# Parameter tables of a state-space convolution built in two halves of the channels, with new instruction lists

## The chip, the cores and the metric

The kernel runs on one core of one Trainium2 chip. The core has five engines that each work through their own row of instructions in order: TensorE (PE, matmuls; the loads of its weights are shown as PEld), VectorE (DVE), ScalarE (ACT), GpSimd (POOL) and SyncE (SP, which here only issues DMA transfers; ACT issues some too). An engine that reaches an instruction whose semaphore has not been raised stands still, with all that is behind it. The metric is the device time of one execution in microseconds; lower is better.

## What is computed

Two independent heads read different inputs of 2048 positions by 448 channels, and their outputs stand side by side. The first is a linear attention of 16 heads with softmax features:

```python
phi_q = jnp.concatenate([_softmax(pq, axis=-1), _softmax(-pq, axis=-1)], axis=-1)
phi_k = jnp.concatenate([_softmax(pk, axis=-1), _softmax(-pk, axis=-1)], axis=-1)
kv = jnp.einsum("bhsf,bhsd->bhfd", phi_k, v)
z  = jnp.einsum("bhsf->bhf", phi_k)
...
o = num / den
```

The second is a state-space convolution. Each of the 448 channels has 256 complex states; they give a convolution kernel of 2048 taps, which is applied through Fourier transforms:

```python
dt = jnp.exp(log_dt)[:, None]
A = A_re + 1j * A_im
...
logdA = dt * A
dB = dt * Bc
...
P = jnp.exp(logdA[:, :, None] * l[None, None, :])
K = jnp.einsum("dn,dnl,dn->dl", Cc, P, dB).real
...
Yf = Uf * Kf[None, :, :, :]
y = (lambda x, s, axes=(-2,-1): jnp.fft.irfft2(x, s=s, axes=axes).astype(jnp.bfloat16))(Yf, (1, L2), axes=(-2, -1))[:, :, 0, :L]
y = (lambda x, *d: x.transpose(*d))(y, 0, 2, 1) + u * Dskip[None, None, :]
```

## The kernel before, in words

**Parameters.** The six raw parameter arrays (A, B, C; real and imaginary) are loaded as bf16 tiles of 112 partitions by 4 x 256 (`raw`, line 260). The 448 channels are split as (u p j): u is the half of the channels (224 each), p the partition, j one of two neighbours. `to_states` (331) multiplies them on PE with the diagonal matrix `DG` of time steps, which also turns them so that the 128 partitions hold states; the results go to a pair of PSUM banks, one for each half of the states. From A come `AT` and `TH` (340 to 349, in two bf16 parts each, by a copy and a difference), and in fp32 the powers of the decay: five exponentials (`amp`), ten sines (`cs`), five products (`PW`, 379) for the powers 128, 16, 8, 32 and 64, and the power 256 by squaring. From B and C come four products of 112 x 1024 (353) and from these the coefficients `CR`, the row for tap 0 (`K0`), and `CB` (`TM`, 389, is the product that it is made of). Each of these instructions covers all 448 channels: 896 columns for each of the real and the imaginary part.

**Tables by quarters.** The rest of the convolution runs in four quarters qt of 112 channels, 224 columns (`QC`). `tables(qt)` makes rotations (sines on ACT), dampings (exponentials on ACT), `hi_tables` and `damp` and `far` (products on DVE), then `build_k` (896 small matmuls over the four quarters) makes the taps, which are sent through DRAM (`scatter_k`) to another layout. `kernel_spectrum(qt)` transforms them on PE, and `conv(qt)` multiplies them on DVE with the signal's spectrum (`prod`, `finish`), transforms back on PE (`inverse`) and writes out.

**Signal and attention.** `signal_spectrum(b)` (419) mirrors u on PE with the constant `REV` (part of the tile `PID`), adds and subtracts on DVE (427, 428), and transforms on PE with the constants `G1`. `key_side` and `query_side` are the attention; they read x transposed by DMA (`xT`), and weights folded by `fold_weights`.

**What sets the order.** The program is collected as a list of some thousand operations, then issued in the order of a fixed list, `ORDER`. Three more lists fix where each tile stands in SBUF (`PLACES`, in units of 64 bytes), which PSUM banks a job uses (`SLOTS`), and which of two engines takes an operation that either could do, or which queue a DMA goes to (`PICKS`: A for ACT and V for DVE; S for SP and Q for ACT's queue). Tiles whose places overlap are kept apart by semaphores: a load into a place waits until the readers of what stood there are done, and whatever is behind it on SP waits too.

Of the kernel before, what the change touches and what calls it, by code (L numbers as in the profile page):

```python
# [19 lines left out]
SSM_N = 256  # L20
# [109 lines left out]
def kernel(  # L130
# [129 lines left out]
    raw = {nm: sb([112, 4, SSM_N]) for nm in srcs}  # L260

    def load_raw(nm):
        dma("S", raw[nm].rearrange("p (u j) n -> p u (j n)", u=2), srcs[nm].rearrange("(u p j) n -> p u (j n)", u=2, j=2))
# [15 lines left out]
    def load_u(b):  # L279
# [9 lines left out]
    prog.add("S", lambda: nc.scalar.dma_start(  # L289
        out=raw["Are"].rearrange("p (u j) n -> p u (j n)", u=2),  # L290
        in_=srcs["Are"].rearrange("(u p j) n -> p u (j n)", u=2, j=2)))
    dma("S", PID, P_d)
    for nm in ("Aim", "Cre", "Bre", "Cim", "Bim"):
        load_raw(nm)
# [30 lines left out]
    def from_states(bs):  # L325
        return view(psum[:, bs[0], 0:1], [512 * (bs[1] - bs[0]), 2], [56, 8], [1, 56])

    def by_states(v):
        return view(v, [56, 2], [112, 8], [1, 56])

    def to_states(bs, terms):
        items = []
        for j in range(4):
            for nch in range(2):
                at = 224 * (j // 2) + 56 * (j % 2)
                o = view(psum[:, bs[nch], at:at + 1], [112, 2], [1, 56])
                items += acc(o, [(t[:, j, 128 * nch:128 * nch + 128], d[:, j, :]) for t, d in terms])
        mms(items)

    AT = sb([128, 2, NCOL])  # L340
    TH = sb([128, 2, NCOL])
    bA, bT = prog.banks(2), prog.banks(2)
    for nm, b, dst in (("Are", bA, AT), ("Aim", bT, TH)):
        to_states(b, [(raw[nm], DG)])
        for nch in range(2):
            o0, o1 = (view(dst[:, part, 56 * nch:56 * nch + 1], [112, 8], [1, 2], [2, 28]) for part in range(2))
            i = view(psum[:, b[nch], 0:1], [56, 8], [28, 2], [1, 28])
            copy(o0, i)
            sub(o1, i, o0)
    prods = {}  # L350
    for a, b in (("Cre", "Bre"), ("Cim", "Bim"), ("Cre", "Bim"), ("Cim", "Bre")):
        prods[a + b] = sb([112, 4, SSM_N])
        mul(prods[a + b], raw[a], raw[b])

    LOWP = (128, 16, 8, 32, 64)
    PW = {k: sb([128, 2, NCOL]) for k in (8, 16, 32, 64, 128, 256)}
    amp = {k: sb([128, NCOL], F32) for k in LOWP}
    cs = {k: sb([128, 2, NCOL], F32) for k in LOWP}
    q128, q256 = (sb([128, 2, NCOL], F32) for _ in range(2))
    CR = sb([128, 2, NCOL])  # L360
    K0 = sb([128, D_MODEL])
    ones = sb([128, 128])
    for k in LOWP:
        af(by_states(amp[k]), from_states(bA), ACT.Exp, scale=float(k))
    for part, terms in enumerate(([("CreBre", DG), ("CimBim", DGN)], [("CreBim", DG), ("CimBre", DG)])):
        bs = prog.banks(2)
        to_states(bs, [(prods[n], d) for n, d in terms])
        copy(by_states(CR[:, part, :]), from_states(bs))
    mset(ones, 2.0 ** -17)
    (b_,) = prog.banks(1)  # L370
    mms([it for qt in range(4) for it in acc(
        view(psum[:, b_, 112 * qt:112 * qt + 1], [14, 8], [7, 2], [1, 7]),
        [(ones, view(CR[:, 0, QC * qt + 56 * nch:QC * qt + 56 * nch + 1], [7, 8], [112, 2], [1, 7]))
         for nch in range(2)])])
    copy(K0, psum[:, b_, 0:D_MODEL])
    for k in LOWP:
        af(by_states(cs[k][:, 0, :]), from_states(bT), ACT.Sin, scale=float(k), bias=bias_hp)
        af(by_states(cs[k][:, 1, :]), from_states(bT), ACT.Sin, scale=float(-k if k == 8 else k))
        mul(PW[k] if k != 128 else q128, cs[k], amp[k].unsqueeze(1).to_broadcast([128, 2, NCOL]))
        if k == 128:  # L380
            copy(PW[128], q128)
    s2 = sb([128, 2, NCOL], F32)
    square(s2, q128)
    sub(q256[:, 0, :], s2[:, 0, :], s2[:, 1, :])
    stt(q256[:, 1, :], q128[:, 0, :], -2.0, q128[:, 1, :], ALU.mult, ALU.mult)
    copy(view(PW[256][:, 0, 0:1], [56, 32], [1, 2], [2, 28]), view(q256[:, 0, 0:1], [56, 32], [28, 2], [1, 28]))
    CB = sb([128, 2, NCOL])
    TM = sb([128, 2, 2, NCOL])
    mul(TM, CR.unsqueeze(1).to_broadcast([128, 2, 2, NCOL]), PW[8].unsqueeze(2).to_broadcast([128, 2, 2, NCOL]))
    add(CB[:, 0, :], TM[:, 0, 0, :], TM[:, 1, 1, :])  # L390
    sub(CB[:, 1, :], TM[:, 0, 1, :], TM[:, 1, 0, :])
# [79 lines left out]
    def args(src, qt):  # L471
        cols = slice(qt * QC, (qt + 1) * QC)
# [23 lines left out]
    def dampings(qt):  # L496
        A = sb([128, 21, QC])
        p0, far_ = args(AT, qt)
# [13 lines left out]
    def damp(W, A, T, qt, x0, w):  # L512
        scaled(A[:, 2:21:3, x0:x0 + w], A[:, 1:20:3, x0:x0 + w], -1.0)
        for part in (1, 0):
            copy(view(W[:, part, 1, x0:x0 + 1], [56, w // 56], [2, 28], [1, 2]),
                 view(PW[8][:, part, qt * QC + x0:qt * QC + x0 + 1], [56, w // 56], [1, 28], [28, 2]))
            mul(view(W[:, part, 2, x0:x0 + 1], [2 * QC, 7], [QC, 2], [1, w]),
                view(A[:, 0, x0:x0 + 1], [3 * QC, 7], [(1 + part) * QC, 2], [1, w]),
                view(T[:, part, 0, x0:x0 + 1], [QC, 7], [0, 2], [1, w]))

    def far(W, qt, x0, w):
        def pw(i, n):
            return view(PW[256][:, i, qt * QC + x0:qt * QC + x0 + 1], [0, 2], [0, n], [1, w])
# [14 lines left out]
        def squares(s0, ka, kb, d0):  # L538
# [3 lines left out]
            for i in range(2):  # L542
# [4 lines left out]
             PW[256][:, :, qt * QC + x0:qt * QC + x0 + w])  # L547
# [6 lines left out]
    def hi_tables(qt):  # L554
        cols = slice(qt * QC, (qt + 1) * QC)
# [5 lines left out]
        copy(U_[:, :, 0], CB[:, :, cols].rearrange("p i (s x) -> p s i x", x=28))  # L561
        for k, n, s0, d0 in ((16, 1, 0, 1), (32, 2, 0, 2), (64, 4, 0, 4)):
            t = sb([128, 2, 8, n, 2, 28])
            for i in range(2):
                times(t[:, i], U_[:, :, s0:s0 + n], PW[k][:, i, cols], 2 * n)
# [3 lines left out]
        for i, o in ((1, t), (0, U_[:, :, 8:16])):  # L569
            times(o, U_[:, :, 0:8], PW[128][:, i, cols], 16)  # L570
# [153 lines left out]
    def kernel_spectrum(qt, tiles):  # L724
        sk = SK[qt]
        for m in range(0, 8, 2):
            for b in range(2):
                (bk,) = prog.banks(1)
                items = []
                for cp in range(2):  # L730
                    for k in range(2):
# [3 lines left out]
                            halves(K0[:, 112 * qt:112 * qt + 112]),  # L735
# [206 lines left out]
```

## Time and profile before

| what | us |
|---|---|
| median of 3 runs (232.2 to 234.28) | 232.46 |
| the profiled execution | 233.31 |
| its span on the page | 231.6 |
| what lies around the span | 1.71 |

The page gives 7313 instructions in 231.6 us, and three engines near their full time: PE 201.2 us (87%), DVE 211.5 (91%), ACT 195.2 (84%). The granted PE clock is below full only between 23 and 35 us. Rows of the busy table by stage show, behind the stretch and its length, busy time and number of instructions for each engine. Rows in order of time show the start, the busy time, the engine, the line, the operation with its shapes, and in brackets the idle time just before and what ended it. Rows of groups show shape and count, then total busy time and the mean of one in ns, then idle time before them. Most lines are helpers: 186 is any DVE operation on two tensors, 206 an activation, 214 a copy on either engine, 229 a matmul, 249 a DMA.

### The profile page before, as it was taken

To read this page: it belongs to the slowest core of one execution; us is meant where nothing else is said; L and a number is where in the kernel's file an instruction comes from. 1 tells how busy PE (TensorE), PEld (TensorE's weight loads), DVE (VectorE), ACT (ScalarE), POOL (GpSimd) and SP (SyncE) were. 2 spreads that over 40 slices of the span, in tenths; PEclk is the share of its full clock that TensorE was granted. 3 is DMA by queue.
4 is the path that set the end of the run, shared out by engine and by line. 5 is a ranking of instruction groups with operands and counts; after the bars stand their busy time and mean duration, and the time that the engine had idled before them with its cause. 6 is when DMAs were issued, how large, how long until landed. Compare 5 with 4: busy or idle time off the path is not lost.

```text
span 231.6 us, 7313 instructions
## 1 busy us (share of the span) xinstructions
PE 201.2 (87%) x3125; PEld 146.0 (63%) x3136; DVE 211.5 (91%) x268; ACT 195.2 (84%) x354; POOL 8.0 (3%) x26
## 2 busy tenths in 40 slices
PE   1115699999999999999886899999999998999994
PEld 1014345656556755797664877745667876789994
DVE  1469999999999999999999999999999996999990
ACT  3977999999999999999999999999699867445331
POOL 4000000000000200002000000010000000000000
PEclk9999569999999999999999999999999999999999
DMA  5918990536828949997755807124799239464173
GB/s 168 214 24 188 290 219 3 128 105 200 215 55 135 229 110 232 143 170 204 238 134 63 233 0 237 32 55 24 181 267 285 52 58 217 86 107 93 25 181 79
DMA packets 78247, 32.87 MB, mean 142 GB/s; under 512 B 64856, under 2 KB 76168, under 8 KB 77960
## 3 DMA queue, kind: packets, MB, share of 16 engines
q1 hardware_dynamic: 72840, 29.76, 59.7%
q10 hardware_dynamic: 5376, 2.65, 4.6%
q8 instruction: 24, 0.39, 0.8%
q14 instruction: 7, 0.06, 0.1%
HBM read 15.84 MB, written 8.49 MB: 105 GB/s over the span
## 4 chain that ended last, share of the span: by engine, by line
PE 58%; ACT 24%; issue 4%; DVE 4%; DVEq 0%; ACTq 0%
PE psum L229 57%; ACT sbuf L206 12%; ACT sbuf L214 11%; DVE sbuf L186 3%; ACT L206 1%; PE psum L239 1%; DVE sbuf L214 0%; DVEq L214 0%; ACTq L214 0%; DVEq L186 0%; ACTq L206 0%
## 5 line engine op out<-in xcount | busy, mean ns | idle before, releaser
L229 PE MATMUL psum<-sbuf 128*128 128x112 bf16 (+9 forms) x3077 | 199.0, 256 | 26.7 <-DVE sbuf L186 10.4
L186 DVE TENSOR_TENSOR sbuf<-sbuf 128x896 bf16<-128x896 bf16 (+11 forms) x214 | 190.9, 955 | 10.4 <-DMA sbuf<-in_B_u_dram 4.6
L229 PEld LDWEIGHTS <-sbuf 128*128 128x128 bf16 (+5 forms) x3088 | 143.5, 113 | 81.1 <-issue 22.6
L214 ACT CAST sbuf<-psum 128x448 bf16<-128x448 f32 (+8 forms) x124 | 79.6, 691 | 21.7 <-PE psum L229 19.1
L206 ACT ACTIVATE sbuf<-psum 128x512 bf16<-128x512 f32 (+6 forms) x154 | 83.1, 625 | 3.2 <-DVE sbuf L186 1.3
L206 ACT ACTIVATE sbuf<-sbuf 128x896 bf16<-128x896 bf16 (+3 forms) x29 | 18.8, 680 | 2.5 <-DMA sbuf<-in_B_log_dt_dram 1.3
L214 DVE CAST sbuf<-psum 128x448 bf16<-128x448 f32 (+4 forms) x21 | 12.2, 597 | 6.3 <-PE psum L229 6.2
L206 ACT ACTIVATE sbuf<-psum,sbuf 128x896 f32<-128x896 f32 (+3 forms) x17 | 13.7, 811 | 1.8 <-DVE sbuf L186 1.3
L224 POOL MEMSET sbuf<- 128x224 bf16 (+7 forms) x21 | 7.6, 388 | 157.1 <-PE psum L229 68.6
L214 ACT COPY sbuf<-psum 112x896 bf16<-112x896 bf16 (+2 forms) x12 | 7.1, 620 | 2.4 <-PE psum L239 1.9
L203 ACT ACT_TABLE_LOAD x5 | 6.4, 1283 | 1.3 <-PEq L926 1.3
L206 ACT ACT_TABLE_LOAD x4 | 5.1, 1283 | 0.1
L214 DVE COPY sbuf<-sbuf 128x448 bf16<-128x448 bf16 (+2 forms) x13 | 4.1, 319 | 0.0
L239 PE MATMUL psum<-sbuf 112*112 112x112 bf16 (+1 forms) x48 | 3.4, 216 | 0.7 <-DVE sbuf L186 0.7
L239 PEld LDWEIGHTS <-sbuf 112*112 112x112 bf16 (+1 forms) x48 | 2.9, 120 | 1.3 <-DVE sbuf L186 0.8
L186 DVE TENSOR_TENSOR sbuf<-psum,sbuf 128x448 bf16<-128x448 f32 (+1 forms) x6 | 2.8, 489 | 0.0
L214 DVE CAST sbuf<-sbuf 128x1792 bf16<-128x1792 f32 (+1 forms) x4 | 2.8, 710 | 0.0
L217 DVE TENSOR_SCALAR sbuf<-sbuf 128x1568 bf16<-128x1568 bf16 x4 | 2.5, 628 | 0.0
L214 ACT COPY sbuf<-sbuf 128x224 bf16<-128x224 bf16 (+1 forms) x5 | 2.2, 443 | 0.0
L220 ACT ACTIVATE sbuf<-sbuf 128x1792 f32<-128x1792 f32 x1 | 1.7, 1702 | 0.0
L217 ACT ACTIVATE sbuf<-sbuf 112x448 bf16<-112x448 bf16 x1 | 0.6, 577 | 0.8 <-DVE sbuf L309 0.8
L198 DVE SCALAR_TENSOR_TENSOR sbuf<-sbuf,psum 128x128 f32<-128x128 f32 x4 | 1.1, 285 | 0.0
(8 smaller groups left out, 2.5 us busy)
## 6 DMA issues: line engine op xcount, KB each, us to landing
SUd<-sbuf SPq DMA_DIRECT2D x8, 448.0 KB, 3.6
sbuf<-SUd SPq DMA_DIRECT2D x4, 896.0 KB, 4.9
sbuf<-const SPq DMA_DIRECT2D x8, 384.0 KB, 3.8
sbuf<-in_B_u_dram SPq DMA_DIRECT2D x4, 448.0 KB, 6.6
out_dram<-sbuf SPq DMA_DIRECT2D x13, 112.0 KB, 2.7
out_dram<-sbuf SPq DMA_DIRECT2D x3, 448.0 KB, 3.5
sbuf<-const SPq DMA_DIRECT2D x2, 512.0 KB
sbuf<-const ACTq DMA_DIRECT2D x1, 1024.0 KB
```

Source lines behind the costliest of these rows:

```text
L186: prog.add("V", lambda: nc.vector.tensor_tensor(out=o, in0=a, in1=b, op=op))
L198: prog.add("V", lambda: nc.vector.scalar_tensor_tensor(out=o, in0=a, scalar=s, in1=b, op0=op0, op1=op1))
L203: nc.scalar.preload_act_table_set("natural_log_exp_and_others")
L206: nc.scalar.activation(o, a, fn, **kw)
L214: either(lambda: nc.scalar.copy(o, a), lambda: nc.vector.tensor_copy(o, a))
L217: either(lambda: nc.scalar.activation(o, a, ACT.Copy, scale=s), lambda: nc.vector.tensor_scalar_mul(o, a, s))
L220: either(lambda: nc.scalar.activation(o, a, ACT.Square), lambda: nc.vector.tensor_tensor(out=o, in0=a, in1=a, op=ALU.mult))
L224: prog.add("G", lambda: nc.gpsimd.memset(o, v))
L229: nc.tensor.matmul(o, lhsT=l, rhs=r, **kw)
L239: nc.tensor.transpose(o, i, idn)
```

## The change

Everything from the raw loads to `CB` becomes a function of the half u, with tiles half as wide, and is called twice. The work of the second half stands behind in the lists. The two halves of the states now lie side by side in one PSUM bank instead of in a pair, so that the exponentials, sines and copies read plain rows. The quarters read the half `qt // 2`. The four lists are new; they also change places, banks, engines and order of operations that the rest of the diff does not touch: `PID` stands at 3415 instead of 370.

```diff
-    raw = {nm: sb([112, 4, SSM_N]) for nm in srcs}
...
+    raw = [{nm: sb([112, 2, SSM_N]) for nm in srcs} for u in range(2)]
...
     for nm in ("Aim", "Cre", "Bre", "Cim", "Bim"):
-        load_raw(nm)
+        load_raw(nm, 0)
+    for nm in srcs:
+        load_raw(nm, 1)
...
+    def to_states(b, u, terms):
+        mms([it for j in range(2) for nch in range(2) for it in acc(
+            view(psum[:, b, 112 * j + 56 * nch:112 * j + 56 * nch + 1], [224, 2], [1, 56]),
+            [(t[:, j, 128 * nch:128 * nch + 128], d[:, 2 * u + j, :]) for t, d in terms])])
...
+    HC = NCOL // 2
+    AT, TH, CR, CB = ([sb([128, 2, HC]) for u in range(2)] for _ in range(4))
+    PW = {k: [sb([128, 2, HC]) for u in range(2)] for k in (8, 16, 32, 64, 128, 256)}
+    K0 = [sb([128, D_MODEL // 2]) for u in range(2)]
...
+    def powers(u):
+        (bA,), (bT,) = prog.banks(1), prog.banks(1)
...
+            prods[a + b] = sb([112, 2, SSM_N])
+            mul(prods[a + b], raw[u][a], raw[u][b])
...
+        for k in LOWP:
+            af(amp[k], psum[:, bA, 0:HC], ACT.Exp, scale=float(k))
...
+        for k in LOWP:
+            af(cs[k][:, 0, :], psum[:, bT, 0:HC], ACT.Sin, scale=float(k), bias=bias_hp)
+            af(cs[k][:, 1, :], psum[:, bT, 0:HC], ACT.Sin, scale=float(-k if k == 8 else k))
+            mul(PW[k][u] if k != 128 else q128, cs[k], amp[k].unsqueeze(1).to_broadcast([128, 2, HC]))
+            if k == 128:
+                copy(PW[128][u], q128)
...
+        TM = sb([128, 2, 2, HC])
+        mul(TM, CR[u].unsqueeze(1).to_broadcast([128, 2, 2, HC]), PW[8][u].unsqueeze(2).to_broadcast([128, 2, 2, HC]))
+        add(CB[u][:, 0, :], TM[:, 0, 0, :], TM[:, 1, 1, :])
+        sub(CB[u][:, 1, :], TM[:, 0, 1, :], TM[:, 1, 0, :])
+
+    powers(0)
+    powers(1)
...
-        p0, far_ = args(TH, qt)
+        p0, far_ = args(TH[qt // 2], qt)
```

In the changed program DVE has 287 operations instead of 268, ACT 372 instead of 354 and PE as many as before; ACT loads a table eleven times instead of nine.

More of the change, by code (lines that the diff above doesn't have):

```diff
@@ L288 @@
     prog.add("G", lambda: nc.gpsimd.affine_select(eye, eye, [[-1, 112]], ALU.is_equal, 0.0, base=0, channel_multiplier=1))
[L289 to L291 removed]
+    prog.add("S", lambda: nc.scalar.dma_start(out=raw_pair("Are", 0)[0], in_=raw_pair("Are", 0)[1]))
     dma("S", PID, P_d)
     for nm in ("Aim", "Cre", "Bre", "Cim", "Bim"):
[L294 removed]
+        load_raw(nm, 0)
+    for nm in srcs:
+        load_raw(nm, 1)
     for i in range(4):
@@ L323, in two @@
         return view(psum[0:parts, bs[0], 0:1], [512 * (bs[1] - bs[0]), 2], [1, D_MODEL])
[L325 to L347, printed above, removed]
+    def to_states(b, u, terms):
+        mms([it for j in range(2) for nch in range(2) for it in acc(
+            view(psum[:, b, 112 * j + 56 * nch:112 * j + 56 * nch + 1], [224, 2], [1, 56]),
+            [(t[:, j, 128 * nch:128 * nch + 128], d[:, 2 * u + j, :]) for t, d in terms])])
@@ new lines @@
+    LOWP = (128, 16, 8, 32, 64)
+    HC = NCOL // 2
+    AT, TH, CR, CB = ([sb([128, 2, HC]) for u in range(2)] for _ in range(4))
+    PW = {k: [sb([128, 2, HC]) for u in range(2)] for k in (8, 16, 32, 64, 128, 256)}
+    K0 = [sb([128, D_MODEL // 2]) for u in range(2)]
+    ones = sb([128, 128])
+    mset(ones, 2.0 ** -17)
+    def powers(u):
+        (bA,), (bT,) = prog.banks(1), prog.banks(1)
+        for nm, b, dst in (("Are", bA, AT[u]), ("Aim", bT, TH[u])):
+            to_states(b, u, [(raw[u][nm], DG)])
+            o0, o1 = (view(dst[:, part, 0:1], [56, 8], [1, 2], [2, 28]) for part in range(2))
+            i = view(psum[:, b, 0:1], [56, 8], [28, 2], [1, 28])
@@ L348 @@
             copy(o0, i)
             sub(o1, i, o0)
[L350 to L391, printed above, removed]
+        prods = {}
+        for a, b in (("Cre", "Bre"), ("Cim", "Bim"), ("Cre", "Bim"), ("Cim", "Bre")):
+            prods[a + b] = sb([112, 2, SSM_N])
+            mul(prods[a + b], raw[u][a], raw[u][b])
@@ new lines, in powers @@
+        amp = {k: sb([128, HC], F32) for k in LOWP}
+        cs = {k: sb([128, 2, HC], F32) for k in LOWP}
+        q128, q256 = (sb([128, 2, HC], F32) for _ in range(2))
+        for k in LOWP:
+            af(amp[k], psum[:, bA, 0:HC], ACT.Exp, scale=float(k))
+        for part, terms in enumerate(([("CreBre", DG), ("CimBim", DGN)], [("CreBim", DG), ("CimBre", DG)])):
+            (b,) = prog.banks(1)
+            to_states(b, u, [(prods[n], d) for n, d in terms])
+            copy(CR[u][:, part, :], psum[:, b, 0:HC])
@@ new lines, in powers @@
+        (b_,) = prog.banks(1)
+        mms([it for q in range(2) for it in acc(
+            view(psum[:, b_, 112 * q:112 * q + 1], [14, 8], [7, 2], [1, 7]),
+            [(ones, view(CR[u][:, 0, QC * q + 56 * nch:QC * q + 56 * nch + 1], [7, 8], [112, 2], [1, 7]))
+             for nch in range(2)])])
+        copy(K0[u], psum[:, b_, 0:D_MODEL // 2])
+        for k in LOWP:
[4 more added lines that the diff above has]
+                copy(PW[128][u], q128)
@@ new lines, in powers @@
+        s2 = sb([128, 2, HC], F32)
+        square(s2, q128)
+        sub(q256[:, 0, :], s2[:, 0, :], s2[:, 1, :])
+        stt(q256[:, 1, :], q128[:, 0, :], -2.0, q128[:, 1, :], ALU.mult, ALU.mult)
+        copy(view(PW[256][u][:, 0, 0:1], [56, 16], [1, 2], [2, 28]), view(q256[:, 0, 0:1], [56, 16], [28, 2], [1, 28]))
+        TM = sb([128, 2, 2, HC])
+        mul(TM, CR[u].unsqueeze(1).to_broadcast([128, 2, 2, HC]), PW[8][u].unsqueeze(2).to_broadcast([128, 2, 2, HC]))
+        add(CB[u][:, 0, :], TM[:, 0, 0, :], TM[:, 1, 1, :])
@@ L560, in hi_tables @@
         U_ = sb([128, 8, N_HI, 2, 28])
-        copy(U_[:, :, 0], CB[:, :, cols].rearrange("p i (s x) -> p s i x", x=28))
+        copy(U_[:, :, 0], CB[qt // 2][:, :, cols].rearrange("p i (s x) -> p s i x", x=28))
         for k, n, s0, d0 in ((16, 1, 0, 1), (32, 2, 0, 2), (64, 4, 0, 4)):
@@ L564, in hi_tables @@
             for i in range(2):
-                times(t[:, i], U_[:, :, s0:s0 + n], PW[k][:, i, cols], 2 * n)
+                times(t[:, i], U_[:, :, s0:s0 + n], PW[k][qt // 2][:, i, cols], 2 * n)
             sub(U_[:, :, d0:d0 + n, 0, :], t[:, 0, :, :, 0, :], t[:, 1, :, :, 1, :])
@@ L569, in hi_tables @@
         for i, o in ((1, t), (0, U_[:, :, 8:16])):
-            times(o, U_[:, :, 0:8], PW[128][:, i, cols], 16)
+            times(o, U_[:, :, 0:8], PW[128][qt // 2][:, i, cols], 16)
         sub(U_[:, :, 8:16, 0, :], U_[:, :, 8:16, 0, :], t[:, :, :, 1, :])
```

28 lines of the change are left out of this document (16 added, 12 removed), and 114 rows, old and new, of tables (ORDER, PLACES, SLOTS).

## The prediction

> **What bounds the kernel now.** I read the busy table by stage first, since three engines are near 90% on the page and only a split by time tells which of them is short where. The stages are cut where VectorE (DVE) changes from waiting to running.
>
> ```profile
> core 0: us, PE busy (x) PEld busy (x) DVE busy (x) ACT busy (x) POOL busy (x), PEclk, DMA share, GB/s
> 0.00:17.50 17.50, 2.63 (x27) 2.50 (x28) 7.01 (x13) 12.55 (x16) 2.56 (x12) 1.00 0.61 134
> 17.50:46.00 28.50, 23.52 (x153) 14.15 (x151) 28.50 (x35) 26.90 (x38) 0.52 (x1) 0.82 0.73 166
> 46.00:79.00 33.00, 32.54 (x395) 19.58 (x394) 33.00 (x39) 32.87 (x56) 0.36 (x2) 1.00 0.68 159
> 79.00:117.00 38.00, 36.26 (x621) 26.27 (x622) 37.81 (x55) 37.29 (x86) 3.28 (x6) 1.00 0.85 181
> 117.00:147.00 30.00, 26.62 (x540) 20.91 (x544) 29.61 (x42) 29.35 (x58) 0.43 (x2) 1.00 0.52 125
> 147.00:187.60 40.60, 39.63 (x537) 27.07 (x539) 40.29 (x48) 36.52 (x67) 0.86 (x4) 1.00 0.59 124
> 187.60:198.00 10.40, 9.49 (x293) 6.73 (x293) 7.40 (x16) 6.49 (x14) 0.00 (x0) 1.00 0.83 153
> 198.00:225.90 27.90, 27.84 (x517) 26.30 (x517) 27.45 (x30) 12.15 (x23) 0.00 (x0) 1.00 0.51 102
> 225.90:231.60 5.70, 2.69 (x55) 2.53 (x52) 0.39 (x1) 1.04 (x3) 0.00 (x0) 0.97 0.38 81
> sum 231.60, PE 201.22 PEld 146.03 DVE 211.46 ACT 195.17 POOL 8.01; mean PE 22.36 PEld 16.23 DVE 23.50 ACT 21.69 POOL 0.89
> ```
>
> DVE is the bound almost everywhere. Its 20.1 us of idle time lie in three places: 10.5 us before 17.5, 3.0 us between 187.6 and 198, 5.3 us at the very end; in the 170.1 us from 17.5 to 187.6 it rests 0.9 us in all. So the time is DVE's work plus those gaps, as long as ScalarE (ACT), which rests under 1 us between 46 and 79 and 1.4 us between 79 and 147, and TensorE (PE), which runs 27.84 of 27.9 us in the tail, do not become later than it. I then read the waits and the order of time at the two ends.
>
> ```profile
> 4.17 0.62 DVE L186 TENSOR_TENSOR sbuf<-sbuf 112x448 bf16<-112x448 bf16 x1 [4.17 <-ACT sbuf L206]
> ...
> 4.85 1.65 PE L229 MATMUL psum<-sbuf 112*128 112x112 bf16 x16 [4.85 <-DVE sbuf L309]
> ...
> 10.40 1.28 ACT L206 ACT_TABLE_LOAD   x1
> 11.69 1.01 ACT L206 ACTIVATE sbuf<-psum,sbuf 128x896 f32<-128x896 f32 x1
> ...
> 13.51 1.29 DVE L186 TENSOR_TENSOR sbuf<-sbuf 112x1024 bf16<-112x1024 bf16 x2 [4.64 <-DMA sbuf<-in_B_u_dram]
> ...
> 15.79 1.28 DVE L186 TENSOR_TENSOR sbuf<-sbuf 112x1024 bf16<-112x1024 bf16 x2
> ...
> 17.10 0.37 SPq L249 DMA_DIRECT2D sbuf<-const  x1
> ...
> 17.53 11.69 DVE L186 TENSOR_TENSOR sbuf<-sbuf 128x1792 bf16<-128x1792 f32 x6
> ...
> 22.24 0.94 PE L229 MATMUL psum<-sbuf 128*128 128x448 bf16 x4 [2.55 <-ACT sbuf L214]
> ...
> 25.35 0.70 ACT L206 ACTIVATE sbuf<-psum,sbuf 128x448 bf16<-128x448 f32 x1
> ```
>
> ```profile
> 30.46 9.54 PE psum L229 x48
> ```
>
> ```profile
> DVE sbuf L214 <- PE psum L229: 4.6, 3, 1.9
> ```
>
> The coefficient products wait for a load until 13.51. The constant PID is placed at 370, inside the raw C_im (370 to 402), so SP can only issue it at 17.10, right after the last products end at 15.79 + 1.28; everything behind it on SP, half of u among it, waits too. PE needs PID for its first signal matmuls (22.24), and the spectrum proper starts at 30.46 in the chain of waits, because DVE's full-width power products (11.69 us from 17.53) stand ahead of the sums that it reads. In the last row, the waits of DVE after 187, the stall in the tail is DVE standing at copies of PSUM that PE has not filled.
>
> **The prices.** These are the groups by shape, for DVE and for ACT. I use busy time by count, which holds the overlap of neighbours.
>
> ```profile
> L186 DVE TENSOR_TENSOR sbuf<-sbuf 128x1792 bf16<-128x1792 bf16 x44 | 46.1, 1094 | 0.1
> ...
> L186 DVE TENSOR_TENSOR sbuf<-sbuf 128x896 bf16<-128x896 bf16 x74 | 43.1, 625 | 0.6
> ...
> L214 DVE CAST sbuf<-psum 128x448 bf16<-128x448 f32 x14 | 8.6, 624 | 1.6 <-PE psum L229 1.6
> L186 DVE TENSOR_TENSOR sbuf<-sbuf 128x1792 bf16<-128x1792 f32 x4 | 7.9, 2022 | 0.0
> ...
> L186 DVE TENSOR_TENSOR sbuf<-sbuf 128x448 bf16<-128x448 bf16 x16 | 5.8, 393 | 0.1
> ...
> L186 DVE TENSOR_TENSOR sbuf<-sbuf 112x1024 bf16<-112x1024 bf16 x4 | 2.6, 684 | 4.6 <-DMA sbuf<-in_B_u_dram 4.6
> ...
> L214 DVE CAST sbuf<-sbuf 128x1792 bf16<-128x1792 f32 x2 | 2.3, 1170 | 0.0
> ...
> L214 DVE CAST sbuf<-psum 128x224 bf16<-128x224 f32 x1 | 0.4, 392 | 1.9 <-PE psum L229 1.9
> ```
>
> ```profile
> L206 ACT ACTIVATE sbuf<-psum 128x448 bf16<-128x448 f32 x44 | 23.5, 605 | 0.2 <-PE psum L229 0.2
> ...
> L206 ACT ACTIVATE sbuf<-psum 128x896 f32<-128x896 f32 x10 | 8.8, 931 | 1.3 <-DVE sbuf L186 1.3
> ...
> L206 ACT ACTIVATE sbuf<-psum,sbuf 128x896 f32<-128x896 f32 x5 | 5.1, 1012 | 1.3 <-DVE sbuf L186 1.3
> ...
> L206 ACT ACTIVATE sbuf<-psum,sbuf 128x448 bf16<-128x448 f32 x4 | 2.6, 655 | 0.0
> ```
>
> **The front.** In the new lists DVE's first operation is the same (4.17, 0.62 us). PE then needs 4 of the former 16 matmuls before DVE's first copy: 4 x 1.65/16 = 0.4 us from 4.85, so about 5.3. From there I add up DVE's row of operations: copy, difference, product, scaling, copy, three products, difference, the first power product at 9.6; ACT feeds that one at 5.7 + 0.53 + 0.65 + 1.28 + 0.53 = 8.7 (two sines, a table, one exponential). The next table load is over at 12.8 and the other eight sines at 17.3, each before DVE asks for it. So DVE runs without a hole to the signal sum at about 20. Idle in front: 4.2 + 0.5, plus what the half loads cost.
>
> ```profile
> sbuf<-in_B_C_re_dram SPq DMA_DIRECT2D x1, 224.0 KB, 5.0
> ```
>
> If a half load still took these 5.0 us, the products asked for at 6.5 and 7.8 and issued by 2.3 and 3.3 would come up to 0.8 and then 0.5 us late; with half the bytes, and nothing but other halves ahead, I expect less. I take 5.1 us idle instead of 10.5: **-5.4 us** (bounds -4.5 and -5.8). PID and u are no longer tied to C_im; PE starts the spectrum at about 21 instead of 30.46. The second halves' loads stand behind on SP; two of them wait for DVE or PE, with transposes of x and weights behind them, but their readers stand tens of us later in the lists, and that cover I price at nothing; if it fails, a transfer of some 5 us is late.
>
> **The work itself.** Halving keeps the elements and adds instructions: DVE goes from 268 to 287. One 1792 costs 46.1/44 = 1.05, two 896 cost 2 x 43.1/74 = 1.16: 0.12 us for each cut. Five power products become ten: +0.6. Four 1024 products (0.65) become eight of 512 (0.40, between the rows of 448 and 1024): +0.6. The other cuts (TM, the sums and differences of CB, q256): +0.7. The two casts of powers, 2.3 us, leave DVE but for one half, 0.65: -1.6. The scaling of DG and three small copies come to DVE: +0.4. The largest item is not the halving but the new choices of engine for copies of PSUM: nine more on DVE (two of 1024, three of 896, two of 448, one of 224, one of 128) and five fewer (three of 448, one of 320, one of 240), which is 4,080 elements and four instructions net. From 224 (0.39) to 448 (8.6/14 = 0.61) an element costs 1.0 ns and an instruction 0.17: 4.1 + 0.7 = +4.7. Sum: **+5.4 us** on DVE, 211.5 to about 216.9. It all lies on the path, since DVE is the bound; nothing hides it. Of it, 5.3 stand ahead of the end of the last quarter's tables.
>
> [...]
>
> **ACT's share.** Fifteen exponentials and sines of 896 (13.9 us) become thirty of 448: 20 x 0.53 + 10 x 0.65 = 17.2, +3.3. Two table loads more, each 1.28 with the next activation at 11.69 right behind it: +2.6. Copies and the scaling that go to DVE give back about 2: **+4 us** on ACT, against some 2 us less idle time in front (4.95 of 17.5 before; first table, the wait for log_dt and for PE, 2.9, after). The first rotation is reached at about 19.2 instead of 25.35 (17.3, and two copies of the mirrored u at the 0.9 to 1.0 of these rows), with half the powers owed. ACT stays off the sum in my forecast, because DVE loses as much.
>
> [...]
>
> **The tail.** The end of the quarter-3 tables stands at 187.6 now. It moves by -5.4 + 5.3, plus new waits in between. The stretch from 17.5 to 187.6 holds 0.9 us of them now; for a list in which DVE copies more from PSUM I add 0.5 (bounds -0.9 and +4): 188.0. From there PE had 9.49 + 27.84 + 2.69 = 40.0 us of work in 44.0. In the new list the fourteen matmul groups of build_k(3) follow each other without the seven groups of query_side and kernel_spectrum that cut them apart now, so their copies, and the transfer of KT(3), come sooner; but these groups follow later, and only one output group and one spectrum group have gone ahead. At the 0.21 us of a 448 and 0.053 of a 112 below that is 0.8 + 0.9:
>
> ```profile
> L229 PE MATMUL psum<-sbuf 128*128 128x448 bf16 x392 | 81.4, 359 | 3.8 <-ACT sbuf L214 3.1 <-issue 0.4
> L229 PE MATMUL psum<-sbuf 128*128 128x112 bf16 x1064 | 56.8, 213 | 1.4 <-ACT sbuf L214 1.1 <-DVE sbuf L214 0.3
> ```
>
> PE keeps 38.3 us; with its 1.0 us of holes and the 3.0 us after its last matmul, 42.3. DVE's own path, 35.2 + 5.3, would be 40.5, so with DVE's stalls gone PE is late next: **-1.7 us** (bounds -3.5 and +1).
>
> **Sum.** -5.4 + 5.3 + 0.5 - 1.7 = -1.3 (the last 0.1 of DVE's 5.4 lies behind the tables, where PE is last): span 230.3, execution 232.0 against its own 233.31. The median of the runs is 232.46, 0.85 lower than the profiled one, so 231.2 there.
>
> **The rivals.** *The head start is kept* (228.5): the half loads cost nothing (-0.4), the middle has no new holes (-0.5), and the tail falls to DVE's path (-1.8): 231.2 - 2.7. For it: PE starts 9 us sooner, and PE rested 3.4 us from 117 to 147, so it can carry work forward. Against: there it waited for others, and the list puts query_side behind build_k. *ACT comes late* (236.5): the second half's ten sines, five exponentials and the table, 5 x 0.53 + 5 x 0.53 + 5 x 0.65 + 1.28 = 9.8 us, come onto ACT in the middle, where it has 1.5 us of holes from 46 to 147. It gets there 25.35 - 19.2 = 6.2 us ahead and so leaves 3.6 us late; if the exponentials of key_side and of the dampings wait in that row and DVE stands behind them, the 3.6 are added, and PE, starved meanwhile, brings all of its backlog into the tail, whose 1.7 us fall away: 231.2 + 5.3. It decides as soon as DVE waits over 2 us for ACT between 46 and 147; for it speaks that ACT rests 0.13 of 33 us there, against it that DVE, too, gets work later. *It does not start sooner* (236.6): the halves land no earlier since u and PID crowd in behind; the front then gives nothing and the work stays, 231.2 + 5.4.
>
> **How the numbers follow.** Forecast 0.36, head start kept 0.32, ACT late 0.26, no earlier start 0.06. Changes within 1% are no change that a measurement of this kernel can tell: 230.1 to 234.8. A small part of the forecast's bounds lies below it. Faster 0.34, within 0.36, slower 0.30. The forecast's own range is 229.6 to 233.6; to hold the time 8 times in 10 it reaches to the rivals on both sides, 227.8 to 236.8.
>
> **What would show it.** Right: DVE busy near 217, idle before 17.5 about 5 us, PID issued near 4.5, PE's spectrum near 21, end of the tables near 188, no stall of DVE at build_k(3). Wrong: DVE busy unchanged (then copies in PSUM cost less), DVE rests over 3 us between 20 and 188, or the products still wait for a load.

## The result and the profile after

The changed kernel takes 231.56 us in the median of 20 runs (230.31 to 232.97). The kernel before, run beside it on the same chip, takes 233.32 (20 runs); the ratio is 0.9943, with a 95% interval of 0.992 to 0.9965. The ratio leaves out executions that are over 1.5% above the fastest of their kernel, so it is not the quotient of these two medians. It makes the changed kernel 1.3 us or 0.57% faster, which lies within the 1% that the prediction took as no change; the forecast was 1.3 us or 0.55%. The profiled execution took 230.66 us, with a span of 228.9 against 231.6 before. It is 0.9 us faster than its own median, and the two profiles lie 2.7 us apart, twice as far as the ratio says.

The whole sum of the two profiles shows in two rows for each kernel, cut where PE begins `build_k(3)`, the end of the quarter-3 tables. The columns are the stretch, its length, busy time and instructions of PE, PEld, DVE, ACT and POOL, the granted PE clock, and DMA. First the kernel before, then the changed one:

```profile
0.00:187.60 187.60, 161.20 (x2265) 110.47 (x2276) 176.22 (x225) 175.49 (x314) 8.01 (x26) 0.97 0.67 149
187.60:231.60 44.00, 40.02 (x861) 35.56 (x860) 35.23 (x45) 19.68 (x40) 0.00 (x0) 1.00 0.57 111
```

```profile
0.00:186.03 186.03, 163.04 (x2292) 109.97 (x2292) 180.22 (x245) 178.12 (x336) 7.60 (x25) 1.00 0.66 148
186.03:228.90 42.87, 38.46 (x845) 34.54 (x844) 35.09 (x43) 18.63 (x37) 0.20 (x1) 1.00 0.65 124
```

Up to the end of the tables DVE works 180.22 us instead of 176.22, 4.0 more, and rests 5.8 instead of 11.4, 5.6 less: the tables end 1.6 sooner. The stretch behind them is 1.1 shorter. Together that is the 2.7 us between the two spans.

In front, in order of time (start, busy time, engine and line, operation, in brackets the idle time before and what ended it):

```profile
3.15 0.43 SPq L249 DMA_DIRECT2D sbuf<-in_B_C_im_dram  x1
...
4.93 0.60 SPq L249 DMA_DIRECT2D sbuf<-const  x1
```

```profile
3.64 0.63 DVE L186 TENSOR_TENSOR sbuf<-sbuf 112x448 bf16<-112x448 bf16 x1 [3.64 <-ACT sbuf L206]
4.88 0.65 DVE L214 CAST sbuf<-psum 128x448 bf16<-128x448 f32 x1 [0.62 <-PE psum L229]
...
5.57 0.66 DVE L186 TENSOR_TENSOR sbuf<-psum,sbuf 128x448 bf16<-128x448 f32 x1
6.12 0.41 DVE L186 TENSOR_TENSOR sbuf<-sbuf 112x512 bf16<-112x512 bf16 x1
...
7.17 1.08 DVE L186 TENSOR_TENSOR sbuf<-sbuf 112x512 bf16<-112x512 bf16 x3
...
8.72 1.08 DVE L186 TENSOR_TENSOR sbuf<-sbuf 128x896 bf16<-128x896 f32 x1
```

PID goes out at 4.93 instead of 17.10. The products stand at 7.17 with no wait before them, and the first power product comes at 8.72 instead of 17.53. DVE rests 3.64 + 0.62 = 4.3 us here instead of 10.5; the other 2.6 of the 8.8 us by which that product comes sooner are less work ahead of it, since the second half's share now stands behind.

The rest by stages, with the tail cut at its last matmul:

```profile
46.00:79.00 33.00, 28.58 (x400) 17.83 (x400) 32.83 (x37) 32.88 (x63) 2.25 (x4) 1.00 0.87 178
79.00:117.00 38.00, 36.33 (x608) 25.98 (x607) 37.39 (x58) 37.94 (x87) 2.30 (x7) 1.00 0.65 148
117.00:147.00 30.00, 28.60 (x526) 21.02 (x529) 29.77 (x37) 29.29 (x58) 0.00 (x0) 1.00 0.37 96
147.00:186.03 39.03, 38.84 (x572) 27.04 (x560) 38.55 (x52) 34.59 (x66) 0.51 (x2) 1.00 0.61 125
...
191.81:225.40 33.59, 33.59 (x616) 29.99 (x616) 29.47 (x35) 14.86 (x28) 0.00 (x0) 1.00 0.64 126
...
sum 228.90, PE 201.51 PEld 144.52 DVE 215.31 ACT 196.75 POOL 7.81; mean PE 22.39 PEld 16.06 DVE 23.92 ACT 21.86 POOL 0.87
```

DVE stays nearly full from 46 to 186, and ACT is as full as DVE up to 147, as it was before. What is new is PE between 46 and 79, with 4.4 us of rest where it had 0.5. From 191.81 PE runs without a hole to its end.

### The profile page after: what moved, and what is told of

Read it like the earlier page. It is cut to its first block, busy times and chain, and to the rows that moved or that the text cites. A ratio compares the mean times of both kernels' runs of the same rounds, so it can differ in the third digit from the quotient of the medians.

```text
span 228.9 us, 7369 instructions
## 1 busy us (share of the span) xinstructions
PE 201.5 (88%) x3136; PEld 144.5 (63%) x3136; DVE 215.3 (94%) x287; ACT 196.8 (86%) x372; POOL 7.8 (3%) x26
## 5 line engine op out<-in xcount | busy, mean ns | idle before, releaser
L229 PE MATMUL psum<-sbuf 128*32 128x80 bf16 (+10 forms) x3088 | 199.5, 255 | 23.2 <-DVE sbuf L186 6.8
L186 DVE TENSOR_TENSOR sbuf<-sbuf 128x896 bf16<-128x896 bf16 (+10 forms) x227 | 192.4, 902 | 5.6 <-ACT sbuf L206 3.8
L206 ACT ACTIVATE sbuf<-psum 128x512 bf16<-128x512 f32 (+6 forms) x164 | 87.8, 638 | 4.1 <-PE psum L229 4.0
L214 DVE CAST sbuf<-psum 128x448 bf16<-128x448 f32 (+5 forms) x24 | 17.1, 712 | 3.8 <-PE psum L229 3.8
L206 ACT ACTIVATE sbuf<-psum,sbuf 128x448 f32<-128x448 f32 (+3 forms) x22 | 15.1, 716 | 0.0
L214 ACT CAST sbuf<-sbuf 128x896 bf16<-128x896 f32 (+1 forms) x5 | 4.4, 880 | 0.0
L214 DVE COPY sbuf<-sbuf 128x224 bf16<-128x224 bf16 (+2 forms) x14 | 3.4, 261 | 0.0
L217 DVE TENSOR_SCALAR sbuf<-sbuf 128x1568 bf16<-128x1568 bf16 (+1 forms) x5 | 2.7, 547 | 0.0
L214 ACT COPY sbuf<-sbuf 128x448 bf16<-128x448 bf16 (+2 forms) x4 | 2.4, 598 | 0.0
L220 ACT ACTIVATE sbuf<-sbuf 128x896 f32<-128x896 f32 x2 | 2.1, 1028 | 0.0
```

The lines of the kernel that those rows point to most:

```text
L186: prog.add("V", lambda: nc.vector.tensor_tensor(out=o, in0=a, in1=b, op=op))
L206: nc.scalar.activation(o, a, fn, **kw)
L214: either(lambda: nc.scalar.copy(o, a), lambda: nc.vector.tensor_copy(o, a))
L217: either(lambda: nc.scalar.activation(o, a, ACT.Copy, scale=s), lambda: nc.vector.tensor_scalar_mul(o, a, s))
L220: either(lambda: nc.scalar.activation(o, a, ACT.Square), lambda: nc.vector.tensor_tensor(out=o, in0=a, in1=a, op=ALU.mult))
L229: nc.tensor.matmul(o, lhsT=l, rhs=r, **kw)
```

## Experiments

The theory at this point: DVE sets the end of the tables, PE the tail; an earlier front is worth its time one to one, and the copies newly put on DVE are the price. The rivals: ACT or PE is the bound of the middle; the untied PID alone brings the gain; the gain is not in the loads at all. Each run (4 to 12 executions) has a ratio to the kernel before, run beside it. Dividing by 0.9943 and taking 231.56 us gives the difference to the changed kernel; the uncertainty of the 0.9943 itself (0.5 us) is not in the brackets.

| run | ratio to before (95%) | against the changed kernel, us |
|---|---|---|
| DVE 7.6 us more in the middle | 1.0198 (1.0138 to 1.0258) | +5.9 (4.5 to 7.3) |
| ACT 7.7 us more in the middle | 1.0284 (1.023 to 1.0338) | +7.9 (6.7 to 9.2) |
| PE 5.8 us more in the middle | 1.0294 (1.0227 to 1.036) | +8.2 (6.6 to 9.7) |
| five PSUM copies back on ACT | 1.0233 (1.0188 to 1.0279) | +6.8 (5.7 to 7.8) |
| PID tied again | 1.0023 (0.9977 to 1.0069) | +1.9 (0.8 to 2.9) |
| kernel before, PID untied | 1.0009 (0.9968 to 1.005) | |
| PE 5.8 us more in the tail | 1.0167 (1.0078 to 1.0256) | +5.2 (3.1 to 7.3) |
| DVE 6.0 us more in the tail | 1.0232 (1.016 to 1.0303) | +6.7 (5.1 to 8.4) |
| exponentials first | 1.01 (1.0065 to 1.0135) | +3.7 (2.8 to 4.5) |
| whole raw loads in front | 1.0009 (0.9977 to 1.0041) | +1.5 (0.8 to 2.3) |
| DVE 3.4 us more in front | 1.0104 (1.0071 to 1.0137) | +3.7 (3.0 to 4.5) |
| one copy sooner | 0.9883 (0.9844 to 0.9922) | -1.4 (-2.3 to -0.5) |

### Which engine is the bound

Six runs issue some operations a second time; the result is the same and nothing else moves in the lists (the two added lines of code move the line numbers of the profile by two: L231 is the matmul here, L188 the DVE operation on two tensors).

```diff
         for i in order:
             self.issue(i)
+            if i in TWICE:
+                self.issue(i)
```

DVE in the middle:

> The changed kernel in which DVE issues four of its products a second time (two of 3136 in the damping of quarter 1, two of 3584 in the table of quarter 2): 2 x 1.78 + 2 x 2.02 = 7.6 us more on DVE between 60 and 140 us, same results. If DVE sets the end of the quarter-3 tables, as my theory has it, and PE has nothing to catch up with behind them, the time rises by 6 to 7.6 us. If PE or ACT is the bound of the middle and DVE's fill of 98% only follows from it, it rises by less than 3.

ACT in the middle:

> The changed kernel in which ACT issues twelve exponentials of 448 of the key side a second time: 12 x 0.65 = 7.7 us more on ACT between 50 and 75 us, same results. If DVE is the bound and ACT has slack to give (4.4 us of rest between 147 and 186), it rises by 0 to 4 us. If ACT is as tight as DVE in the middle (the rival of the late ACT), by 6 to 7.7.

PE in the middle:

> The changed kernel in which PE issues seven groups of four 448 matmuls of the key side a second time: 7 x 0.83 = 5.8 us more on PE between 45 and 65 us, same results. PE rested 4.4 us between 46 and 79 and 3.3 between 79 and 186. If only DVE is the bound there, 0 to 2 us more. If PE is what everything follows, 4.5 to 5.8.

For DVE 5.9 is just under the theory's 6 to 7.6, with the interval reaching into it. For ACT and PE the theory failed: it had up to 4 and up to 2 us, and 7.7 us of ACT cost 7.9, as by the rival, and 5.8 us of PE even 8.2, more than the rival's 4.5 to 5.8. The waits of DVE between 46 and 90 us say how, first with ACT's work doubled, then with PE's (who waited for whom; us in total, times, longest):

```profile
DVE sbuf L188 <- PE psum L231: 3.5, 1, 3.5
DVE sbuf L188 <- ACT sbuf L208: 3.3, 3, 2.2
DVE sbuf L216 <- PE psum L231: 0.9, 1, 0.9
```

```profile
DVE sbuf L188 <- ACT sbuf L208: 3.3, 2, 1.8
DVE sbuf L188 <- PE psum L231: 2.3, 1, 2.3
```

In each run DVE loses 5.6 to 7.7 us, in part to the engine that was loaded and in part to the other. In the changed kernel DVE rests 0.2 us between 46 and 79. So DVE's fill of 99% does not make it the only bound: in this list the three engines are tied, and none has slack to give here. The list stays as it was made for the changed kernel; what another order would do with the added work was not tried. The 4.4 us that PE rests between 46 and 79 are no reserve: nearly all are waits for ACT, and work put on PE elsewhere does not fill them.

```profile
PE psum L229 <- ACT sbuf L214: 3.8, 4, 2.0
```

PE's 8.2 need not all be the price of its work. In the trace of that run the tables end at 191.80 instead of 186.03, 5.8 us later. Behind that PE stands for 2.5 us, and the profile shows nothing that it waited for ("issue"):

```profile
198.29 0.66 PE L231 MATMUL psum<-sbuf 128*32 128x80 bf16 x24 [2.49 <-issue]
```

The four executions of the run took 238.68, 239.23, 241.13 (the profiled one) and 241.27 us. Whether this stand is what sets the two pairs apart is not shown.

The same in the tail:

> The changed kernel in which PE issues three inverse groups a second time, 3 x 1.9 = 5.8 us more on PE behind 195 us, same results. If PE is the bound of the tail, as forecast, 5 to 6 us more; if DVE's path is, under 3.

> The changed kernel in which DVE issues three products of 3584 of the third convolution a second time, 3 x 2.0 = 6.0 us more on DVE behind 192 us, same results. DVE rests 2.7 us there while PE has no hole. If PE is the bound of the tail and DVE is 2 us behind it, 2 to 4 us more; if both are tight, 5 to 6; if DVE is far off the path, under 1.

PE's share came as the theory had it. DVE's cost all that was added, and with 6.7 (5.1 to 8.4) perhaps more, though it rests 4.1 us between 191.81 and 225.40 in the changed kernel. PE's row in order of time with DVE's work doubled:

```profile
193.22 15.04 PE L231 MATMUL psum<-sbuf 128*128 128x448 bf16 x270 [0.84 <-ACT sbuf L216]
212.91 21.14 PE L231 MATMUL psum<-sbuf 128*128 128x112 bf16 x346 [4.65 <-DVE sbuf L216]
```

PE stands 4.65 us for a PSUM bank that DVE is to empty: the copy waits in DVE's row behind the doubled products. With this stand comes a clock of 0.50 from 211.59 to 218.42, and PE's same 616 matmuls take 36.2 us of busy time instead of 33.6. So the tail, too, is both engines': DVE's copies of PSUM bind PE to the order of DVE's row.

### The copies that went to DVE

```diff
 PICKS, by the copy that they are for:
-signal_spectrum(1): ur[:, 2:4] V, the two of sg for k = 3 V V    query_side(0): the two of OT V V
+signal_spectrum(1): ur[:, 2:4] A, the two of sg for k = 3 A A    query_side(0): the two of OT A A
```

> The changed kernel with five of the PSUM copies that it put on DVE (three of 896, two of 1024) back on ACT: DVE 3.2 + 2.4 = 5.6 us less, ACT some 5.1 us more. If DVE's added copies are the price of this change and ACT has room, the time falls by 2 to 5 us. If ACT is as tight as DVE, it stays within 1 us or rises by up to 4.

The time rises by 6.8 us although DVE has 5.6 us less to do. DVE's waits between 15 and 60 us:

```profile
DVE sbuf L186 <- ACT sbuf L206: 3.7, 2, 2.8
DVE sbuf L186 <- ACT sbuf L214: 2.0, 1, 2.0
DVE sbuf L186 <- ACT sbuf L220: 0.6, 1, 0.6
```

They are all for ACT. So the work that the new lists put on DVE, the largest item of the forecast's cost, is what keeps ACT on time in this list. Taken as a cost by itself it is there; taken back it costs more. The places of the copies in the list stay as they are: the first of them starts at 24.66 on ACT, behind a table load and two activations, where DVE starts it at 21.45. A list made for these copies on ACT was not tried.

### Where the head start comes from

Is an earlier DVE in front worth its time?

> The changed kernel in which DVE issues six operations of the front a second time (four products of 512, the first power product, the product TM): 4 x 0.36 + 1.08 + 0.9 = 3.4 us more on DVE between 6 and 12 us, same results. If an earlier DVE in front is worth its time one to one at the end, as the sum took it, the time rises by 3 to 3.8 us. If ACT or PE holds the front, by less than 1.5.

It is: 3.4 us there cost 3.7 (3.0 to 4.5).

Does PID's place bring it? In the changed kernel, C_im's first half goes to PID's place and PID's load behind the products; and in the kernel before, C_im goes to a place of its own.

```diff
-PLACES: PID 3415, C_im(0) 2046        ORDER: ... load of PID, products of C_im ...
+PLACES: PID 3415, C_im(0) 3415        ORDER: ... products of C_im, load of PID ...
```

> The changed kernel with the first half of C_im loaded to PID's place and PID's load behind the four products that read it, as in the kernel before; halves, queues and lists else as they are. PID is then issued at about 9 us instead of 4.93, and u's halves stand behind it on SP. If PE's early start matters, PE's spectrum moves from 20.5 to about 25 and the time rises by 2 to 4 us. If the front is DVE's alone (its first power product at 8.72 needs neither PID nor u), by less than 1.

```diff
-PLACES: PID 370, C_im 370
+PLACES: PID 370, C_im 877
```

> The kernel before with C_im at a place of its own, so that PID's load waits for nothing: PID issued near 5 us instead of 17.1, all else as before. If PID was what held the front, PE's spectrum comes some 8 us sooner than 30.46 and the time falls by 1 to 4 us. If the halves are what helps (DVE's products wait for the loads until 13.51 either way), DVE's idle time in front stays at 10 to 11 us and the time stays within 1 us.

Tied again, PE's first signal matmul waits for PID:

```profile
15.99 9.94 PE L229 MATMUL psum<-sbuf 128*128 128x448 bf16 x48 [6.84 <-DMA sbuf<-const]
```

It starts at 15.99 instead of 12.07, and the time rises by 1.9 us, just under the 2 to 4 that were expected if PE's early start matters. But untied in the kernel before, PID goes out at 5.25 instead of 17.10 and the time does not move: 1.0009. There DVE still stands until 13.83, and the signal's sums wait behind its full-width products:

```profile
13.83 1.29 DVE L186 TENSOR_TENSOR sbuf<-sbuf 112x1024 bf16<-112x1024 bf16 x2 [4.99 <-DMA sbuf<-in_B_u_dram]
...
17.86 11.69 DVE L186 TENSOR_TENSOR sbuf<-sbuf 128x1792 bf16<-128x1792 f32 x6
```

So the untied PID is worth nothing alone; once DVE has come forward, tying it again costs 1.9 us.

Is it the bytes? The first six raw loads bring whole arrays again, with the work by halves unchanged; the extra half is read by nobody.

```diff
-    raw = [{nm: sb([112, 2, SSM_N]) for nm in srcs} for u in range(2)]
+    whole = {nm: sb([112, 2, 2, SSM_N]) for nm in srcs}
+    raw = [{nm: whole[nm][:, 0] for nm in srcs}, {nm: sb([112, 2, SSM_N]) for nm in srcs}]
...
+        if u == 0:
+            return (whole[nm].rearrange("p u j n -> p u (j n)"),
+                    srcs[nm].rearrange("(u p j) n -> p u (j n)", u=2, j=2))
```

> The changed kernel in which each of the first six raw loads brings the whole array again, as in the kernel before (the second half goes to a place that nobody reads; the second halves are loaded later as they are now). The work of every engine and the lists are unchanged; only the bytes ahead of the products double. If the head start comes from the bytes, the products wait for C_im and B_im until about 12 to 13 us, DVE's idle time in front grows by 4 to 5 us and the time rises by 3.5 to 5.5. If it comes from the smaller products, scalings and sines (computing by halves), DVE's front grows by less than 1.5 us and the time by less than 2.

The answer lies between the two expectations: DVE's idle time grows by more than 1.5 and less than 4 us, and the time by 1.5, under 2. DVE's front in that run:

```profile
4.13 0.62 DVE L186 TENSOR_TENSOR sbuf<-sbuf 112x448 bf16<-112x448 bf16 x1 [4.13 <-ACT sbuf L206]
...
7.18 0.42 DVE L186 TENSOR_TENSOR sbuf<-sbuf 112x512 bf16<-112x512 bf16 x1 [0.46 <-DMA sbuf<-in_B_B_re_dram]
...
9.67 1.10 DVE L186 TENSOR_TENSOR sbuf<-sbuf 112x512 bf16<-112x512 bf16 x3 [1.31 <-DMA sbuf<-in_B_C_im_dram]
...
11.23 1.08 DVE L186 TENSOR_TENSOR sbuf<-sbuf 128x896 bf16<-128x896 f32 x1
```

With whole arrays the products wait for C_im until 9.67, not until 13.51 as in the kernel before, and DVE rests 4.13 + 0.62 + 0.46 + 1.31 = 6.5 us: the whole arrays take back 2.3 of the 6.2 us, and the first power product is 2.5 later. The rest is in the queue: in the kernel before, C_im stands on ACT's queue, behind ACT's first activations, and it goes out after the first loads of u on SP:

```profile
3.87 1.32 SPq L249 DMA_DIRECT2D sbuf<-in_B_u_dram  x2
...
4.84 0.35 ACTq L249 DMA_DIRECT2D sbuf<-in_B_C_im_dram  x1
```

The new `PICKS` send it on SP at 3.15, ahead of u. The packets in the traces agree. In the kernel before, the raw loads on SP are through at 7.04 us, u's packets move from 5.96 to 12.42, and C_im's, on ACT's queue, only from 8.96 to 12.82. With whole arrays in the new order all six arrays are through at 8.15. That this accounts for the other 3.8 us of the wait is read from these traces; C_im moved ahead of u in the kernel before was not tried.

### Two attempts at a better order

ACT loads two tables more than before. All five exponentials of the first half ahead of its first sines save both:

```diff
-ORDER: ... sin 8, sin 8, exp 8, ... exp 64, exp 16, exp 128, product 8, ... exp 32, sin 16 ...
+ORDER: ... exp 8, exp 64, exp 16, ... exp 128, ... exp 32, sin 8, sin 8, product 8, ... sin 16 ...
```

> The changed kernel with all five exponentials of the first half ahead of its first pair of sines (one tile of them at another place for that), so that ACT loads two tables less, 2 x 1.28 = 2.6 us. The first power product then waits for sines behind five exponentials and comes at about 9.5 instead of 8.72 us, 0.8 us lost on DVE. If ACT is as tight as DVE (as the doubled exponentials said, 7.9 us for 7.7), ACT gains some 1.7 to 2.6 and the time falls by 1 to 2 us. If DVE alone sets the time, it rises by about 0.8.

It costs 3.7 us. The first power product comes at 11.84 instead of the expected 9.5:

```profile
11.84 1.09 DVE L186 TENSOR_TENSOR sbuf<-sbuf 128x896 bf16<-128x896 f32 x1 [2.48 <-ACT sbuf L206]
```

because ACT now stands for DVE: 2.05 us ahead of its first exponential of A, 0.72 ahead of the next, 0.79 ahead of the table load for the sines.

```profile
5.54 0.54 ACT L206 ACTIVATE sbuf<-psum 128x448 f32<-128x448 f32 x1 [2.05 <-DVE sbuf L313]
6.80 1.85 ACT L206 ACTIVATE sbuf<-psum 128x448 f32<-128x448 f32 x4 [0.72 <-DVE sbuf L186]
9.44 1.28 ACT L206 ACT_TABLE_LOAD   x1 [0.79 <-DVE sbuf L186]
```

These are the places where ACT reads a PSUM bank of A (its real or its imaginary part) that DVE, ahead of it in the list, reads too: each time ACT goes on 0.03 to 0.08 us after a DVE operation on A's banks ends. The changed kernel's list has them in another order. The expectation had counted ACT's durations and not these waits. DVE's front is 3.1 us later, and the end 3.7 (2.8 to 4.5): that agrees with the doubled work in front, 3.7 for 3.4, and the saved table loads are not seen. Whether they would help without the waits stays open.

The last run moves one pair of operations:

```diff
-ORDER: ... sin of rotations(1), sin 8, build_k matmuls, copy of their bank ...
+ORDER: ... build_k matmuls, copy of their bank, sin of rotations(1), sin 8 ...
```

> The changed kernel with one pair of its lists moved: the last matmul group of the second build_k of quarter 0 and ACT's copy of its PSUM bank go ahead of two sines, so that the copy starts at about 68.8 instead of 70.04 us and PE's longest hole behind 46 us (1.98, waiting for that copy) shrinks to about 0.5. In the changed kernel's other traces a clock of 0.50 follows this hole for some 3.4 us, and DVE then waits 1.2. If the hole brings the low clock and the low clock brings DVE's wait, the clock stays at 1.00 between 70 and 80 and the time falls by 0.5 to 1.3 us against the changed kernel. If the low clock has another cause, it comes as before and the time stays within 0.4 us.

The time falls to 231.16 us in the median against 233.45 for the kernel before, 0.9883 (0.9844 to 0.9922): 1.4 us below the changed kernel by the ratios. That is the lowest ratio here, though its interval touches that of the changed kernel. The mechanism is not shown. The hole behind `build_k` shrinks to 0.71, but the profiled execution, the slowest of the eight at 234.38 us, has another behind it:

```profile
66.64 2.06 PE L229 MATMUL psum<-sbuf 128*32 128x80 bf16 x72 [0.93 <-ACT sbuf L214]
69.40 1.31 PE L229 MATMUL psum<-sbuf 112*128 112x112 bf16 x12 [0.71 <-ACT sbuf L214]
73.93 6.37 PE L229 MATMUL psum<-sbuf 128*128 128x32 bf16 x49 [3.22 <-DMA sbuf<-sbuf]
```

and the low clock comes there too (a mean of 0.83 from 70 to 80 us). For the mechanism speaks only that four of the run's eight executions were granted a mean clock of 0.991 to 0.993 and took 230.2 to 230.8 us, the other four 0.978 to 0.985 and 231.5 to 234.4. The changed kernel's executions, its profiled one apart, have 0.978 to 0.985.

## Why the prediction was right

The ratio moved by the 1.3 us that were forecast, and in part that is luck. Term by term the two profiles give -6.2 + 4.0 + 0.6 - 1.1 = -2.7 where -1.3 was forecast: the front gave 0.8 more and DVE's work cost 1.3 less, both in the kernel's favour, and the tail gave 0.6 less. The profiled execution is one of the faster ones of the changed kernel. In the two traces that double work in the tail the tables end 1.3 and 1.7 us later than in it; executions like these would bring the 2.7 back near 1.3. So the four terms have the right signs and the right order of size, but that their errors came to nothing in the median was not foreseen.

**The front**, forecast -5.4. DVE rests 4.3 us there instead of 10.5, -6.2, with the first power product at 8.72 (forecast 9.6) and PID at 4.93 (4.5). The size is a little over its bounds (-4.5 and -5.8), the reason half right. The bytes are 2.3 us of it; the larger part is, as the traces read, C_im's new place in the queues. The prediction read the row of the wait until 13.51 and named the load, but not that it stood on ACT's queue behind u. PID's place, which the prediction names beside it, held PE and not DVE, and the untied kernel before shows that by itself it was worth nothing.

**DVE's work**, forecast +5.4, +5.3 of it ahead of the tables' end; measured 215.31 - 211.46 = +3.85 and +4.0. The groups agree with the forecast: over PSUM copies alone 12.2 us became 17.1 (the first row is of the kernel before)

```profile
L214 DVE CAST sbuf<-psum 128x448 bf16<-128x448 f32 (+4 forms) x21 | 12.2, 597 | 6.3 <-PE psum L229 6.2
L214 DVE CAST sbuf<-psum 128x448 bf16<-128x448 f32 (+5 forms) x24 | 17.1, 712 | 3.8 <-PE psum L229 3.8
```

which is +4.9 where 4.7 was worked out (a copy of 128 in another group adds 0.3). Four of the five power products became 8.5 from 7.9 and the fifth 2.2 from 2.0, +0.8 where 0.6 was forecast. All groups by shape together are 5.1 us more, 229.2 for 224.1. What was mis-sized is the overlap. In the front's rows above the difference at 5.57 takes 0.66 us, and the product behind it starts at 6.12, 0.11 before that ends. Between neighbours of different shapes such an overlap stands in both groups, but only once in the engine's busy time. This double count is 224.1 - 211.46 = 12.6 us before and 229.2 - 215.31 = 13.9 after, so 1.25 us of the 5.1 are not there. The forecast said that busy time by count holds the overlap of neighbours; it does so only within one group.

**Cuts.** Two f32 products of 896 take 2 x 1.086 us where one of 1792 took 2.022: 0.15 for a cut. About 0.08 of it is overlap with the neighbour: in a row of them the next one starts 1.94 us after a product of 1792 and 1.00 after one of 896, so a cut costs the engine about 0.07.

```profile
L186 DVE TENSOR_TENSOR sbuf<-sbuf 128x896 bf16<-128x896 f32 x8 | 8.5, 1086 | 0.0
```

**ACT**, forecast +4: measured +1.6 of busy time. Its sines and exponentials take 18.2 us in their groups for 13.9, and the tables 2.6 more, no less than worked out; how the rest of the difference splits between copies and overlap is not worked out here. That ACT "stays off the sum" was wrong as a reason. Added work on it costs no less than on DVE (7.9 us for 7.7 in the middle, where DVE's 7.6 cost 5.9), and the copies that DVE took over, which the prediction counted as cost, keep it on time (five of them back on ACT cost 6.8 us).

**New waits in the middle**, forecast +0.5: in the profiled execution DVE rests 1.5 us from 20 to 186 where it rested 0.9 before (17.5 to 187.6), +0.6. The end of the tables was to be at 188.0 and is at 186.03 there. In the two runs that double work in the tail alone, with the same lists up to there, `build_k(3)` begins at 187.3 and 187.7; the last section shows the difference.

**The tail**, forecast -1.7, measured -1.1. PE has 38.46 us of work behind the end of the tables where 38.3 were worked out, and 0.9 us of holes, all before 191.81, where 1.0 was taken. The missing 0.6 is 0.2 of work and the stretch behind the last matmul, 3.5 instead of 3.0. That PE alone is late there, with DVE 1.8 us behind it, was wrong: 6.0 us more on DVE cost 6.7.

**The rivals.** Of the head start kept (228.5) one condition came true, the cheap half loads; but the middle has new waits, and the tail fell to PE and DVE together. ACT late (236.5) did not come, yet it was nearer than the 0.26 suggests: the doubled exponentials (7.9 us for 7.7) show that each us by which ACT were late would have cost about one. No earlier start (236.6) is ruled out by the front's rows.

## What to carry to other kernels

An engine that is full for 99% of a stage is not yet the bound: load another by a known amount before you call its work free, for here 7.6 us more on DVE cost 5.9, 7.7 on ACT 7.9, and 5.8 on PE 8.2, in a list that was not made anew. Price a moved copy together with what it takes from the engine that it leaves. And when a wait for a load ends late, read which queue it was issued on and what stood ahead of it, before its bytes are blamed.

## What the runs showed of the hardware

PE's granted clock differs between executions of the same lists (a mean of 0.978 to 1.00 over the twenty of the changed kernel), and what that costs depends on who stands behind PE. The kernel with DVE doubled in the tail has the changed kernel's lists up to there; its stages around 70 us, and below them those of the changed kernel's profiled execution:

```profile
69.00:71.00 2.00, 0.34 (x8) 0.34 (x7) 2.00 (x3) 2.00 (x5) 0.23 (x1) 1.00 1.48 97
71.00:72.00 1.00, 1.00 (x9) 0.34 (x5) 1.00 (x3) 1.00 (x3) 0.00 (x0) 0.82 1.24 274
72.00:75.00 3.00, 2.44 (x21) 1.18 (x21) 3.00 (x3) 2.37 (x6) 0.00 (x0) 0.50 0.72 201
75.00:76.00 1.00, 1.00 (x19) 0.71 (x18) 0.67 (x1) 0.23 (x1) 0.00 (x0) 0.97 1.05 318
76.00:77.00 1.00, 1.00 (x9) 0.50 (x6) 0.13 (x1) 1.00 (x3) 0.00 (x0) 1.00 0.03 7
```

```profile
69.00:71.00 2.00, 0.25 (x6) 0.24 (x6) 2.00 (x3) 2.00 (x5) 0.32 (x2) 1.00 1.23 121
71.00:72.00 1.00, 1.00 (x11) 0.44 (x7) 1.00 (x3) 1.00 (x3) 0.00 (x0) 1.00 1.10 246
72.00:75.00 3.00, 2.68 (x40) 1.70 (x40) 3.00 (x3) 3.00 (x9) 0.00 (x0) 1.00 0.74 216
```

PE rests in the same place in both. In one, the clock then falls to 0.50 for some 3.4 us; PE gets fewer matmuls done (21 instead of 40 from 72 to 75), ACT then stands 1.4 us for PE and DVE 1.2 for ACT. In the other it stays at 1.00. The next `build_k` begins 1.3 us later with the low clock, at 103.73 instead of 102.43. The same trace has an earlier low clock from 20.45 to 23.86 and loses nothing by it: its first `build_k` begins at 61.33 us, that of the changed kernel at 61.43. The kernel before has its low clock from 23.0 to 33.2 us, where DVE is busy throughout. In the times of whole executions the price does not stand out: of the changed kernel's nineteen others, three with a clock of 0.982 to 0.985 took 230.3 to 230.6 us, no more than the profiled one at 1.00. The clock records of the fourteen traces here have the clock fall 25 times ahead of the last matmul, for 3.41 us each time or two or three times that. PE need not have rested long ahead of a fall: in the 3.41 us before it PE's longest rest is 1.96 us in the trace above (the fall at 71.64), and 1.0 us, with 1.7 and 1.8 of rest in all, in two others (exponentials first; kernel before, PID untied). What brings a fall on is not shown.
